# Attention and token-mixing MLP in one kernel: zeroing by DMA and q, k order at the head; DMA latencies in the scheduler's model and matmul order at the tail

## The chip, the cores and the metric

One core of a Trainium2 chip. The metric is device time in microseconds (us), median of several executions. Beside it stands the *span* of the profiler's record, from the first to the last instruction, about 1.8 to 2.2 us shorter. Engines: PE is TensorE, ACT ScalarE, DVE VectorE, POOL GpSimd, SP the queue that issues nearly all DMAs.

## The reference, cut to what matters

```python
xn = layernorm(x)                                  # x: (1, 2048, 512), bf16
qkv = xn @ wqkv                                    # 32 heads of 16
p = softmax(q @ k^T / 4); o = p @ v; A = o @ wo
u = gelu(einsum("bsd,sf->bdf", layernorm(xn), w1) + b1)   # mixes tokens, F = 1376
B = transpose(einsum("bdf,fs->bds", u, w2) + b2)
return x + A + B
```

The scores make 32 heads x 2048 x 2048 exponentials, worked off as 1024 tiles of 128 x 1024.

## The kernel before

The kernel has its own scheduler. It runs through a model of the engines with a cost for every instruction, and from it decides which engine takes which tile and in what order each engine's instructions stand. The order is then fixed; on the chip semaphores alone decide when things start. A tile's exponential is either one ACT instruction, or on DVE an integer approximation of four terms (one from PSUM, three shifts on DVE or POOL). PE sums `P @ V` with the "PV matmuls": a tile from ACT is one group of four 32-column matmuls, a tile from DVE four groups. "PE's backlog" below is what PE still has to do once the last scores are made.

There are 32 blocks of 32 tiles. After each block DVE copies its sums out; DMAs regroup them and the denominators, DVE takes reciprocals, two more DMA steps spread them, and DVE multiplies. Block 31 at the end takes a short way with 32 x 32 transposes.

The head, cut:

```python
sc.add("dve", lambda e: e.memset(v17_main[:, :, 16:17], 1.0), ...)
sc.add("dve", lambda e: e.memset(wo_t[:], 0.0), ..., cost=(0.92, 0.97))
...
for t in range(NPRE):                 # NPRE = 4 tiles of x
    transpose_pe(t, TB[t]); warm_up(N_MID[t], 5)
for t in range(NPRE):
    transpose_copy(t, TB[t], "dve" if t == 2 else "act")
ln_stats(NPRE)
for t in range(NPRE):
    qt0_tile_pe(t)
    if t == 0: kt_tile_pe(0, t, PV_BANK); kt_tile_evac(0, t, PV_BANK, "dve")
    if t == 1: qt0_evac(0, "dve")
for t in range(1, NPRE): kt_tile_pe(0, t, PV_BANK)
qt0_evac(1, "act")
```

DMA in the model, and the tail, cut:

```python
DMA_I, DMA_L, DMA_SLACK = 0.65, 3.0, 0.8        # issue, latency, slack before a use
...
for sti in range(4): heads_of(2, sti)           # pair 14's output matmuls
warm_up(6, ...)
for half in range(2):
    for sti in (half, half + 2):                # block 31's, needs oL of this half
        for a in range(2): matmul(bank(tbk[sti]), lhsT=oL[...], rhs=wo_t[...])
    for sti in (half, half + 2): heads_of(3, sti)     # block 30's
for sti in (0, 2, 1, 3): # DVE (sti 3: ACT) evacuates, DMA out
```

The softmax here doesn't subtract the row's maximum and nothing guards it: scores larger than these inputs give would overflow.

Of the kernel before, what the change touches and what calls it, by code (L numbers as in the profile page):

```python
# [49 lines left out]
N_MID = (1, 1, 1, 2)  # L50
# [4 lines left out]
PER_LIST = 16  # L55
LN2_AT = 12
PIECE_MIN = 6
PIECE_OPEN = 1
HOLD_MAX = 2.0
PE_LAT = 0.40  # L60
# [7 lines left out]
DMA_SLACK = 0.8  # L68
EXT_SLACK = 0.2
# [7 lines left out]
D_BACK = 0.5  # L77
D_STEAL = 0.3
D_LATE = 0.5
P_KEEP = 4  # L80
DEAD_SLACK = 0.1
PAIR_WAIT = 0.0
# [8 lines left out]
LATE_BY = 0  # L91
# [3 lines left out]
FIN_END = 985  # L95
FIN_STEP = 18
# [26 lines left out]
class Sched:  # L123
    ENGS = ("pe", "act", "dve", "pool", "sp")

    def __init__(self, nc, es):
        self.nc = nc
        self.es = es
        self.streams = {e: [] for e in self.ENGS}
        self.order = []  # L130
        self.last_writer = {}
        self.readers = {}
        self.dma_ops = []
        self.free = {e: 0.0 for e in self.ENGS}
        self.busy = {e: 0.0 for e in self.ENGS}
        self.pe_mode = None
        self.pe_end = 0.0
        self.pe_tiles = {}
        self.phase = 0
        self.pieces = {}  # L140
        self.pe_log = []
        self.port_iv = {"dve": [], "pool": []}
        self.port_op = None

# [38 lines left out]
    def _time(self, op, cost, ready, port):  # L183
# [3 lines left out]
        if op.is_dma:  # L187
            op.t0 = max(self.free[eng], ready)
            self.free[eng] = op.t0 + cost[0]
            op.t1 = op.t0 + cost[1]  # L190
# [148 lines left out]
def bass_parallel_sum__softmax_full_mha__mixer_token_mlp__prompt_kernel(  # L339
# [18 lines left out]
    with ExitStack() as es:  # L358
# [70 lines left out]
        def dma(q, dst, src, reads, writes, name="", noncontig=False, out_dma=False):  # L429
            if noncontig:  # L430
                def fn(eng, dst=dst, src=src):
                    with nc.allow_non_contiguous_dma(reason="tiny strided vector load"):
                        return eng.dma_start(dst, src)
            else:
                def fn(eng, dst=dst, src=src):
                    return eng.dma_start(dst, src)  # L436
            return sc.add(q, fn, reads=reads, writes=writes, name=name, dma=True, out_dma=out_dma)
# [13 lines left out]
        sc.add("dve", lambda e: e.memset(wo_t[:], 0.0), writes=[("wo_t", z) for z in range(4)], cost=(0.92, 0.97))  # L451
# [98 lines left out]
        def ln_norm(t):  # L550
            sc.add("dve", lambda e: e.tensor_scalar(xn_sb[:, t, :], x_sb[:, t, :], mv[:, t, 0:1], mv[:, t, 2:3],
                                                    ALU.subtract, ALU.mult),
                   reads=[("x", t), ("mv", t)], writes=[("xn", t)], cost=(0.3, 0.39))
# [114 lines left out]
        for t in range(NPRE):  # L668
            transpose_pe(t, TB[t])
            warm_up(N_MID[t], 5)  # L670
        for t in range(NPRE):
            transpose_copy(t, TB[t], "dve" if t == 2 else "act")
        ln_stats(NPRE)
        for t in range(NPRE):
            qt0_tile_pe(t)
            if t == 0:
                kt_tile_pe(0, t, PV_BANK)
                kt_tile_evac(0, t, PV_BANK, "dve")
            if t == 1:
                qt0_evac(0, "dve")  # L680
        for t in range(1, NPRE):
            kt_tile_pe(0, t, PV_BANK)
        qt0_evac(1, "act")
# [6 lines left out]
        ln_norm(NPRE)  # L690

        def block0_work(period):
            if period == 0:
                for t in range(NPRE):
                    vt_tile_pe(t, 0, 5, t)
                vt_evac(list(range(NPRE)), 0, 5, "dve")
# [19 lines left out]
            if ok(period + 5):  # L716
                ln_stats(period + 5)
            if ok(period + 4) and period:
                ln_norm(period + 4)
# [303 lines left out]
        def task_epilogue(b):  # L1023
            p, e_ = divmod(b, 2)
            qb, T = PAIRS[p]
            eb, tb_ = b % 2, p % 2
            yield "gate", lambda: b < 2 or b - 2 in ot_free
            yield "pvev", [dict(eng="dve", fn=lambda e: e.tensor_copy(OT32[:, eb, :], bank(PV_BANK)),  # L1028
                                reads=[("bank", PV_BANK)], writes=[("OT32", eb)])]
            for c in range(4):  # L1030
                yield "sp", [dict(dst=dcomp[32 * c:32 * c + 32, eb, :],
                                  src=OT32[32 * c + 16:32 * c + 17, eb, :].rearrange("o (c x) -> o c x", x=16),
                                  reads=[("OT32", eb)], writes=[("dcomp", eb, c)], name="den_in")]
# [3 lines left out]
            else:  # L1037
                yield from task_o_in(b)
            yield "dve", [dict(eng="dve", fn=lambda e: e.reciprocal(rcomp[:, eb, :], dcomp[:, eb, :]),
                               reads=[("dcomp", eb, r) for r in range(4)], writes=[("rcomp", eb)], cost=(0.2, 0.25))]  # L1040
            yield "sp", [dict(dst=rden_d[eb].rearrange("(p x) -> p x", x=16), src=rcomp[:, eb, :],
                              reads=[("rcomp", eb)], writes=[("rden_d", eb)], name="den_mid")]
            for r in range(4):
# [5 lines left out]
                                  reads=[("rden_d", eb)], writes=[("denb", tb_, e_, r)], name="den_out")]  # L1049
# [9 lines left out]
            for h in range(2):  # L1059
# [5 lines left out]
                    writes=oT_keys(qb, T) + [("oTh", h)], port=True, cost=(0.33, 0.41))]  # L1065
# [33 lines left out]
        def tail():  # L1099
# [6 lines left out]
            def heads_of(Tm, sti):  # L1106
                sc.add("pe", lambda e: e.matmul(
                    bank(tbk[sti]), lhsT=oT(qb)[:, Tm, 128 * sti:128 * (sti + 1)], rhs=wo_c[:, Tm, :],
                    start=Tm == 2 and sti < 3, stop=Tm == 3),
# [3 lines left out]
            warm_up(6, 2 * slots[1] + 1, wo_c[:, 0, :], wk)  # L1113
            for half in range(2):
                for sti in (half, half + 2):
                    h = sti // 2
                    for a in range(2):
                        sc.add("pe", lambda e, sti=sti, h=h, a=a, half=half: e.matmul(
                            bank(tbk[sti]), lhsT=oL[:, 256 * a + 128 * half:256 * a + 128 * half + 128],
                            rhs=wo_t[:, 2 * h + a, :], start=False, stop=False),  # L1120
                            reads=[("oTl", half)] + [("wo_t", c) for c in range(4)], writes=[("bank", tbk[sti])])
                for sti in (half, half + 2):
                    heads_of(3, sti)
# [145 lines left out]
        def est(specs, slack=0.0):  # L1269
            s0 = specs[0]  # L1270
            r = 0.0
            for s_ in specs:
                r = max(r, sc.ready(s_["eng"], s_["reads"], s_["writes"], slack=slack, dma_slack=DMA_SLACK))
# [28 lines left out]
        def pieces():  # L1302
# [12 lines left out]
            for tries in range(2):  # L1315
# [21 lines left out]
                if len(g["steps"]) >= PIECE_MIN and len(g["open"]) < PIECE_OPEN and g["steps"][-1][1]:  # L1337
# [27 lines left out]
        while True:  # L1365
            cands = []
# [77 lines left out]
            if cur_ext and cur_ext["cur"] and cur_ext["cur"][0] == "hold" and (next_n >= NN or not score_has(next_n)):  # L1444
# [77 lines left out]
            elif kind == "dma":  # L1522
                w = what["cur"][1][0]
                dma("sp", w["dst"], w["src"], w["reads"], w["writes"], w["name"], out_dma=w.get("out_dma", False))
# [133 lines left out]
```

## Time and profile before

| | before |
|---|---|
| device time, median of 3 | 691.98 us (691.9 to 692.06) |
| span of the profile | 690.4 us (its execution took 692.2) |
| ACT: first exponential starts, last one ends | 12.52, 681.87 |
| exponential tiles on ACT, on DVE | 715, 309 |
| final transpose of block 31 starts on DVE | 682.28 |

Read these as four stretches that add up to the span: the head to the first exponential (12.52), ACT's exponentials (669.35, with the GELU between them), from the last one's end to the final transpose (0.41), and the rest (8.12). ACT is nearly gapless in the second; so a stretch gets shorter only if ACT has less to do, or if what is serial at the ends gets shorter.

### The profile page before, as it was taken

The page shows a single profiled execution, that of the slowest core. Times are in us where ns is not written, and L with a number is a line of the kernel's source. Part 1 is how long each engine was busy: PE and PEld are TensorE (multiplying, and loading weights), DVE is VectorE, ACT ScalarE, POOL GpSimd, SP SyncE. Part 2 cuts the span into 40 slices and gives each one's busy share as a digit, 9 for nine tenths or more (in the row PEclk, how much of TensorE's full clock was granted, in tenths as well). Part 3 has the DMA queues.
Part 4 walks back from the last instruction along what each step waited for, and adds up shares of the span by engine and source line. Part 5 has one row for each costly group of instructions (what it writes and reads, how often), then busy time and mean ns, then how long its engine had stood idle before and what let it go on. Part 6 is the DMA issues. An engine that isn't in the chain of part 4 may idle for free.

```text
span 690.4 us, 29398 instructions
## 1 busy us (share of the span) xinstructions
PE 674.3 (98%) x12934; PEld 309.7 (45%) x12934; DVE 618.7 (90%) x895; ACT 672.3 (97%) x734; POOL 401.7 (58%) x690
## 2 busy tenths in 40 slices
PE   7999999999999999999999999999999999999998
PEld 4534544435444454444444444444444444444444
DVE  7989899998889989889999989898998988888987
ACT  5999999999999999999999999999999999999995
POOL 4536557563455756656666576665665665654643
PEclk9999999999999999999999999999999999999999
DMA  7402001221002200022220212222221222313201
GB/s 214 101 5 54 21 18 21 50 45 29 19 18 50 48 20 19 23 52 49 49 42 20 58 29 55 53 55 55 49 49 34 58 53 57 70 28 87 47 22 48
DMA packets 85728, 32.32 MB, mean 47 GB/s; under 512 B 67424, under 2 KB 85600, under 8 KB 85600
## 3 DMA queue, kind: packets, MB, share of 16 engines
q1 hardware_dynamic: 85168, 30.05, 19.1%
q8 instruction: 101, 1.65, 1.1%
q10 hardware_dynamic: 432, 0.39, 0.2%
q14 instruction: 27, 0.22, 0.1%
HBM read 21.76 MB, written 2.35 MB: 35 GB/s over the span
## 4 chain that ended last, share of the span: by engine, by line
PE 78%; ACT 13%; DVE 5%; issue 1%; POOL 1%; SPq 0%; DMA 0%; DVEq 0%
PE ps L811 32%; PE ps L744 28%; PE ps L842 14%; ACT pT L768 10%; ACT x_sb L768 2%; PE ps L896 1%; DVE pT L779 1%; DVE OT L1028 1%; ACT gT_sb L953 1%; DVE hx L567 1%; DVE oT L1061 0%; SPq L436 0%; DMA denb<-rden_scratch 0%; POOL mv L563 0%; PE ps L648 0%
## 5 line engine op out<-in xcount | busy, mean ns | idle before, releaser
L768 ACT ACTIVATE pT<-ps 128x1024 bf16<-128x1024 f32 x535 | 521.1, 1126 | 2.7 <-PE ps L744 2.1
L779 DVE TENSOR_SCALAR pT<-ps 128x1024 int16<-128x1024 f32 x222 | 271.2, 1222 | 28.0 <-PE ps L744 21.2
L744 PE MATMUL ps<-QT,KT 32*128 32x512 bf16 x2048 | 283.1, 384 | 6.0 <-ACT pT L768 3.0
L785 POOL INT64_ADD pT<-pT x319 | 193.0, 613 | 117.1 <-DVE pT L788 77.5
L811 PE MATMUL ps<-pT,V 128*32 128x256 bf16 x4728 | 249.4, 276 | 3.5 <-DVE OT L1028 3.1
L768 ACT ACTIVATE x_sb<-ps 128x1024 bf16<-128x1024 f32 x180 | 194.0, 1130 | 0.6 <-PE ps L744 0.5
L744 PEld LDWEIGHTS ps<-QT,KT 32*128 32x128 bf16 x2048 | 78.2, 91 | 183.7 <-ACT pT L768 69.8
L811 PEld LDWEIGHTS ps<-pT,V 128*32 128x32 bf16 x4728 | 110.3, 96 | 87.3 <-issue 68.8
L785 POOL INT64_ADD x_sb<-pT x142 | 86.6, 613 | 70.0 <-DVE pT L788 32.2
L811 PE MATMUL ps<-x_sb,V 128*32 128x256 bf16 x1840 | 116.4, 275 | 0.7 <-DVE OT L1028 0.4
L779 DVE TENSOR_SCALAR x_sb<-ps 128x1024 int16<-128x1024 f32 x87 | 106.3, 1221 | 8.8 <-PE ps L744 6.7
L785 POOL INT64_ADD pT<-x_sb x115 | 70.1, 618 | 45.7 <-DVE pT L788 27.9
L788 DVE TENSOR_SCALAR pT<-pT 128x1024 int16<-128x1024 int16 x148 | 62.9, 427 | 4.3
L811 PE MATMUL ps<-pT,VM 128*32 128x256 bf16 x888 | 61.6, 274 | 0.0
L842 PE MATMUL ps<-gT_sb,wblk 128*32 128x512 bf16 (+1 forms) x704 | 61.2, 383 | 0.0
L811 PEld LDWEIGHTS ps<-x_sb,V 128*32 128x32 bf16 x1840 | 46.4, 96 | 29.4 <-issue 23.4
L842 PE MATMUL ps<-hx,wblk 128*32 128x512 bf16 x598 | 52.2, 383 | 0.0
L785 POOL INT64_ADD x_sb<-x_sb x55 | 33.4, 612 | 21.7 <-DVE pT L788 11.9
L850 PE MATMUL ps<-hx,wblk 32*128 32x512 bf16 (+1 forms) x92 | 35.6, 387 | 0.0
L788 DVE TENSOR_SCALAR pT<-x_sb 128x1024 int16<-128x1024 int16 x65 | 27.3, 427 | 1.8
L811 PEld LDWEIGHTS ps<-pT,VM 128*32 128x32 bf16 x888 | 23.4, 96 | 9.5 <-issue 8.2
L788 DVE TENSOR_SCALAR x_sb<-pT 128x1024 int16<-128x1024 int16 x57 | 23.9, 420 | 1.5
(111 smaller groups left out, 449.1 us busy)
## 6 DMA issues: line engine op xcount, KB each, us to landing
wblk<-in_B_w_dram SPq DMA_DIRECT2D x10, 512.0 KB, 4.5
wblk<-in_B_w_dram SPq DMA_DIRECT2D x16, 320.0 KB, 3.5
oC<-OT SPq DMA_DIRECT2D x248, 16.0 KB, 1.8
denb<-rden_scratch SPq DMA_DIRECT2D x124, 32.0 KB, 2.3
xr<-in_A_x_dram SPq DMA_DIRECT2D x16, 128.0 KB, 3.5
dcomp<-OT SPq DMA_DIRECT2D x124, 2.0 KB, 1.7
QT<-Qall SPq DMA_DIRECT2D x120, 16.0 KB, 1.8
out_dram<-osb SPq DMA_DIRECT2D x14, 128.0 KB, 2.0
```

Of the source, the lines that this page charges most:

```text
L567: return [dict(eng="dve", fn=lambda e: e.tensor_scalar(xn_sb[:, t, :], xn_sb[:, t, :], mv[:, t, 3:4], None, ALU.mult), reads=[("xn", t), ( ...
L744: specs.append(dict(eng="pe", fn=lambda e, r=r, bk=bk: e.matmul(bank(bk), lhsT=KT[32 * r:32 * r + 32, T, 128 * kt:128 * (kt + 1)], rhs=QT[ ...
L768: return [dict(eng="act", fn=lambda e: e.activation(buf(pbuf[n]), ps[:, s_ * 1024:(s_ + 1) * 1024], ACTF.Exp, scale=LN2_128), reads=[("ban ...
L779: return dict(eng="dve", fn=lambda e: e.tensor_scalar(buf_i(w), ps[:, s_ * 1024:(s_ + 1) * 1024], IBIAS, 0.0, ALU.add, ALU.max), reads=[(" ...
L785: return dict(eng=eng, fn=lambda e: e.int64_add(buf_i(o).bitcast(I64), buf_i(w).bitcast(I64), SHIFTS[k] * 0x0001000100010001), reads=[("pT ...
L788: return dict(eng=eng, fn=lambda e: e.tensor_scalar(buf_i(o), buf_i(w), float(SHIFTS[k]), 1.0, ALU.add, ALU.mult), reads=[("pT", w)], writ ...
L811: specs.append(dict(eng="pe", fn=lambda e, c=c, h=h, i=i, off=off: e.matmul(bank(PV_BANK)[32 * c:32 * c + 32, 256 * par:256 * par + 256], ...
L842: specs.append(dict(eng="pe", fn=lambda e, c=c, w=w: e.matmul(bank(EX_BANK)[32 * c:32 * c + w, :], lhsT=lhs_of(32 * c, 32 * c + w), rhs=rh ...
L850: return [dict(eng="pe", fn=lambda e: e.matmul(bank(EX_BANK)[0:dst_rows, :], lhsT=lhs_of(0, dst_rows)[rs], rhs=rhs[rs], start=begin, stop= ...
L896: return [dict(eng="pe", fn=lambda e, ct=ct, c=c: e.matmul(bank(EX_BANK)[32 * c:32 * c + 32, 128 * i:128 * (i + 1)], lhsT=xnT[:, ct, 128 * ...
L953: yield "act", [dict(eng="act", fn=lambda e, ap=ap: e.activation(ap, ap, ACTF.Gelu_apprx_tanh), reads=[("gT", f) for f in fts], writes=[(" ...
L1028: yield "pvev", [dict(eng="dve", fn=lambda e: e.tensor_copy(OT32[:, eb, :], bank(PV_BANK)), reads=[("bank", PV_BANK)], writes=[("OT32", eb)])]
```

## The change

Intent: take the zeroing of `wo_t` off DVE at the start, let q and k of the first tile run ahead of later transposes, tell the scheduler more truthful DMA latencies, and at the end give block 30's chain short latencies and keep row pieces (matmuls cut in four by rows, slipped in among the scores) away from the last scores.

```diff
-N_MID = (1, 1, 1, 2)
+N_MID = (1, 0, 0, 1)
+PIECE_STOP = 4
+DMA_SLACK_RCP = 1.5
+DMA_SLACK_OT = 2.5
+DMA_BIG = 5.2
+DMA_Q = 2.4
-            op.t1 = op.t0 + cost[1]
+            op.t1 = op.t0 + max(cost[1], DMA_BIG - (op.t0 - self.big))   # self.big: last w1 or w2 load
-        sc.add("dve", lambda e: e.memset(wo_t[:], 0.0), ...)
+        def zero_wo_t():            # in period 4 of block 0, from a zeroed part of QT
+            dma("sp", wo_t[:], QT[:, 3:4, :].to_broadcast([128, 4, 512]), ...)
@@ head: copy right after each transpose; tile 0's q and k after transpose 1
+            if t == 1: qt0_tile_pe(0); kt_tile_pe(0, 0, PV_BANK)
+        for t in range(1, NPRE - 1): qt0_tile_pe(t)
+        qt0_tile_pe(NPRE - 1)
+        kt_tile_evac(0, 0, PV_BANK, "dve"); qt0_evac(0, "act"); qt0_evac(1, "act")
@@ epilogue of a block
+            quick = b == NBLK - 2;  dc = (DMA_I, DMA_Q) if quick else None    # cost of its DMAs
+            dma_slack=0.0 if quick else DMA_SLACK if b >= NBLK - 4 else DMA_SLACK_RCP (or _OT)
@@ pieces: only while next_n < NN - PIECE_STOP
@@ tail
             warm_up(6, ...)
+            for sti in range(4): heads_of(3, sti)
             for half in range(2): ... # block 31's eight matmuls, with no heads_of(3) between
```

(Cut: ten sets of scheduling rules, all chosen as set 0, which has the old constants; a rule that lets other PE work go before held pieces; names and unused switches.)

More of the change, by code (lines that the diff above doesn't have):

```diff
@@ L55 @@
 PER_LIST = 16
+SEG = 8
+RULES = (
+    (0.5, 0.5, 0.3, 0.0, 6, 0),
+    (0.3, 0.5, 0.3, 0.0, 6, 0),
+    (0.8, 0.5, 0.3, 0.0, 4, 0),
+    (0.5, 0.8, 0.3, 0.0, 6, 0),
+    (0.5, 0.5, 0.45, 0.15, 6, 0),
+    (0.5, 0.5, 0.15, 0.0, 4, 0),
+    (0.5, 0.35, 0.3, 0.3, 4, 0),
+    (0.8, 0.8, 0.3, 0.0, 99, 0),
+    (0.5, 0.5, 0.3, 0.0, 4, 6),
+    (0.5, 0.8, 0.45, 0.1, 4, -6),
+)
+RULE_OF = "00000000000000000000000000000000000000000000000000000000000000000000000000000000000000000000000000000000000000000000000000000000"
 LN2_AT = 12
-PIECE_MIN = 6
 PIECE_OPEN = 1
 HOLD_MAX = 2.0
+ZERO_AT = 4
+POOL_NORM = ()
+STATS_LEAD = 0
+N_LAST = 0
+Q0_ENG = "act"
 PE_LAT = 0.40
@@ L76 @@
 D_FLY = 3
-D_BACK = 0.5
-D_STEAL = 0.3
-D_LATE = 0.5
 P_KEEP = 4
 DEAD_SLACK = 0.1
-PAIR_WAIT = 0.0
 PORT_SLACK = 0.5
@@ L90 @@
 HARD_HOLD = 10
-LATE_BY = 0
 EX_FROM = 34
@@ L143, in __init__ @@
         self.port_op = None
+        self.big = -9.0
     def _deps(self, eng, reads, writes, dma):
@@ L189, in _time @@
             self.free[eng] = op.t0 + cost[0]
-            op.t1 = op.t0 + cost[1]
+            op.t1 = op.t0 + max(cost[1], DMA_BIG - (op.t0 - self.big))
+            if op.name in ("ld_w1", "ld_w2a"):
+                self.big = op.t0
         elif eng == "pe":
@@ L427, in bass_parallel_sum__softmax_full_mha__mixer_token_mlp__prompt_kernel, with dma @@
         H_KEYS = [("xn", t) for t in range(NT)]
-        def dma(q, dst, src, reads, writes, name="", noncontig=False, out_dma=False):
+        def dma(q, dst, src, reads, writes, name="", noncontig=False, out_dma=False, cost=None):
             if noncontig:
@@ L436, in fn @@
                     return eng.dma_start(dst, src)
-            return sc.add(q, fn, reads=reads, writes=writes, name=name, dma=True, out_dma=out_dma)
+            return sc.add(q, fn, reads=reads, writes=writes, name=name, dma=True, out_dma=out_dma, cost=cost)
         sc.add("pool", lambda e: e.memset(ident[:], 0.0), writes=[("ident",)], cost=(0.25, 0.3))
@@ L450, in bass_parallel_sum__softmax_full_mha__mixer_token_mlp__prompt_kernel @@
         sc.add("dve", lambda e: e.memset(v17_main[:, :, 16:17], 1.0), writes=[("Vone",)], cost=(0.5, 0.55))
-        sc.add("dve", lambda e: e.memset(wo_t[:], 0.0), writes=[("wo_t", z) for z in range(4)], cost=(0.92, 0.97))
         sc.add("pool", lambda e: e.memset(qmask[:, 0:1], 0.0), writes=[("qmask",)], cost=(0.1, 0.2))
@@ L550, in ln_norm @@
         def ln_norm(t):
-            sc.add("dve", lambda e: e.tensor_scalar(xn_sb[:, t, :], x_sb[:, t, :], mv[:, t, 0:1], mv[:, t, 2:3],
+            pool = t in POOL_NORM
+            sc.add("pool" if pool else "dve", lambda e: e.tensor_scalar(xn_sb[:, t, :], x_sb[:, t, :], mv[:, t, 0:1], mv[:, t, 2:3],
                                                     ALU.subtract, ALU.mult),
-                   reads=[("x", t), ("mv", t)], writes=[("xn", t)], cost=(0.3, 0.39))
+                   reads=[("x", t), ("mv", t)], writes=[("xn", t)], cost=(2.09, 2.2) if pool else (0.3, 0.39), port=pool)
         def ln2_stats():
@@ L669, in bass_parallel_sum__softmax_full_mha__mixer_token_mlp__prompt_kernel @@
             transpose_pe(t, TB[t])
+            transpose_copy(t, TB[t], "dve" if t == 2 else "act")
             warm_up(N_MID[t], 5)
-        for t in range(NPRE):
-            transpose_copy(t, TB[t], "dve" if t == 2 else "act")
-        ln_stats(NPRE)
-        for t in range(NPRE):
-            qt0_tile_pe(t)
-            if t == 0:
-                kt_tile_pe(0, t, PV_BANK)
-                kt_tile_evac(0, t, PV_BANK, "dve")
-            if t == 1:
-                qt0_evac(0, "dve")
+            if t == 1:
+                qt0_tile_pe(0)
+                kt_tile_pe(0, 0, PV_BANK)
+        for t in range(1, NPRE - 1):
+            qt0_tile_pe(t)
+        warm_up(N_LAST, 5)
+        qt0_tile_pe(NPRE - 1)
+        kt_tile_evac(0, 0, PV_BANK, "dve")
+        qt0_evac(0, Q0_ENG)
+        qt0_evac(1, "act")
+        ln_stats(NPRE)
         for t in range(1, NPRE):
             kt_tile_pe(0, t, PV_BANK)
-        qt0_evac(1, "act")
         evac("dve", KT[:, 0, 128:512], bank(PV_BANK)[:, 128:512], reads=[("bank", PV_BANK)],
@@ L690, in bass_parallel_sum__softmax_full_mha__mixer_token_mlp__prompt_kernel @@
         ln_norm(NPRE)
+        for t in range(NPRE + 1, NPRE + 1 + STATS_LEAD):
+            ln_stats(t)
+        def zero_wo_t():
+            dma("sp", wo_t[:], QT[:, 3:4, :].to_broadcast([128, 4, 512]),
+                reads=[("QT", 3, r) for r in range(4)], writes=[("wo_t", z) for z in range(4)], name="zero")
         def block0_work(period):
+            if period == ZERO_AT:
+                zero_wo_t()
             if period == 0:
@@ L715, in block0_work @@
                 vt_tile_pe(period + 2, 0, 5, period % 2)
-            if ok(period + 5):
-                ln_stats(period + 5)
-            if ok(period + 4) and period:
+            if ok(period + 5 + STATS_LEAD):
+                ln_stats(period + 5 + STATS_LEAD)
+            if ok(period + 5) and period + 5 in POOL_NORM:
+                ln_norm(period + 5)
+            if ok(period + 4) and period and period + 4 not in POOL_NORM:
                 ln_norm(period + 4)
@@ L1026, in task_epilogue @@
             eb, tb_ = b % 2, p % 2
+            quick = b == NBLK - 2
+            dc = (DMA_I, DMA_Q) if quick else None
             yield "gate", lambda: b < 2 or b - 2 in ot_free
@@ L1032, in task_epilogue @@
                                   src=OT32[32 * c + 16:32 * c + 17, eb, :].rearrange("o (c x) -> o c x", x=16),
-                                  reads=[("OT32", eb)], writes=[("dcomp", eb, c)], name="den_in")]
+                                  reads=[("OT32", eb)], writes=[("dcomp", eb, c)], name="den_in", cost=dc)]
             g_in = dict(gen=task_o_in(b), cur=None)
@@ L1039, in task_epilogue @@
             yield "dve", [dict(eng="dve", fn=lambda e: e.reciprocal(rcomp[:, eb, :], dcomp[:, eb, :]),
-                               reads=[("dcomp", eb, r) for r in range(4)], writes=[("rcomp", eb)], cost=(0.2, 0.25))]
+                               reads=[("dcomp", eb, r) for r in range(4)], writes=[("rcomp", eb)], cost=(0.2, 0.25), dma_slack=0.0 if quick else DMA_SLACK if b >= NBLK - 4 else DMA_SLACK_RCP)]
             yield "sp", [dict(dst=rden_d[eb].rearrange("(p x) -> p x", x=16), src=rcomp[:, eb, :],
-                              reads=[("rcomp", eb)], writes=[("rden_d", eb)], name="den_mid")]
+                              reads=[("rcomp", eb)], writes=[("rden_d", eb)], name="den_mid", cost=dc)]
             for r in range(4):
@@ L1048, in task_epilogue @@
                                   src=src.to_broadcast([16, 2, 256]),
-                                  reads=[("rden_d", eb)], writes=[("denb", tb_, e_, r)], name="den_out")]
+                                  reads=[("rden_d", eb)], writes=[("denb", tb_, e_, r)], name="den_out", cost=dc)]
             half = b == NBLK - 2
@@ L1064, in task_epilogue @@
                           [("denb", tb_, x, r) for x in es_ for r in range(4)],
-                    writes=oT_keys(qb, T) + [("oTh", h)], port=True, cost=(0.33, 0.41))]
+                    writes=oT_keys(qb, T) + [("oTh", h)], port=True, cost=(0.33, 0.41),
+                                   dma_slack=0.0 if quick else DMA_SLACK if b >= NBLK - 4 else DMA_SLACK_OT)]
             yield "call", lambda: oT_done.add((qb, T))
@@ L1108, in heads_of @@
                     bank(tbk[sti]), lhsT=oT(qb)[:, Tm, 128 * sti:128 * (sti + 1)], rhs=wo_c[:, Tm, :],
-                    start=Tm == 2 and sti < 3, stop=Tm == 3),
+                    start=Tm == 2 and sti < 3, stop=False),
                     reads=[("oTc", qb, 2) if Tm == 2 else ("oTh", sti // 2)] + wk, writes=[("bank", tbk[sti])])
@@ L1113, in tail @@
             warm_up(6, 2 * slots[1] + 1, wo_c[:, 0, :], wk)
+            for sti in range(4):
+                heads_of(3, sti)
             for half in range(2):
@@ L1119, in tail @@
                             bank(tbk[sti]), lhsT=oL[:, 256 * a + 128 * half:256 * a + 128 * half + 128],
-                            rhs=wo_t[:, 2 * h + a, :], start=False, stop=False),
+                            rhs=wo_t[:, 2 * h + a, :], start=False, stop=a == 1),
                             reads=[("oTl", half)] + [("wo_t", c) for c in range(4)], writes=[("bank", tbk[sti])])
-                for sti in (half, half + 2):
-                    heads_of(3, sti)
             for sti in (0, 2, 1, 3):
@@ L1272, in est @@
             for s_ in specs:
-                r = max(r, sc.ready(s_["eng"], s_["reads"], s_["writes"], slack=slack, dma_slack=DMA_SLACK))
+                r = max(r, sc.ready(s_["eng"], s_["reads"], s_["writes"], slack=slack, dma_slack=s_.get("dma_slack", DMA_SLACK)))
             t = max(sc.free[s0["eng"]], r)
@@ L1336, in pieces @@
                         break
-                if len(g["steps"]) >= PIECE_MIN and len(g["open"]) < PIECE_OPEN and g["steps"][-1][1]:
+                if len(g["steps"]) >= piece_min and len(g["open"]) < PIECE_OPEN and g["steps"][-1][1] and next_n < NN - PIECE_STOP:
                     g["open"].append((g["steps"].pop(-1)[1], {0, 1, 2, 3}))
@@ L1365, in bass_parallel_sum__softmax_full_mha__mixer_token_mlp__prompt_kernel @@
         while True:
+            D_LATE, D_BACK, D_STEAL, PAIR_WAIT, piece_min, LATE_BY = RULES[int(RULE_OF[min(next_n, NN - 1) // SEG])]
             cands = []
@@ L1443, in bass_parallel_sum__softmax_full_mha__mixer_token_mlp__prompt_kernel @@
                 jobs.append((max(t_c, est(cur_ext["cur"][1], EXT_SLACK)), 1 if late > -LATE_BY else 3, "ext", cur_ext, 0.214))
-            if cur_ext and cur_ext["cur"] and cur_ext["cur"][0] == "hold" and (next_n >= NN or not score_has(next_n)):
+            held = cur_ext and cur_ext["cur"] and cur_ext["cur"][0] == "hold" and (next_n >= NN or not score_has(next_n))
+            if held and jobs and min(j[0] for j in jobs) < max(max(sc.piece_ready(r) for o in cur_ext["open"] for r in o[1]), t_pe) + 0.2:
+                held = False
+            if held:
                 for o in cur_ext["open"]:
@@ L1523, in bass_parallel_sum__softmax_full_mha__mixer_token_mlp__prompt_kernel @@
                 w = what["cur"][1][0]
-                dma("sp", w["dst"], w["src"], w["reads"], w["writes"], w["name"], out_dma=w.get("out_dma", False))
+                dma("sp", w["dst"], w["src"], w["reads"], w["writes"], w["name"], out_dma=w.get("out_dma", False), cost=w.get("cost"))
                 step_gen(what)
```

## The prediction

> **What bounds the kernel now.** I first read busy time by engine, then who waits for whom on ScalarE, then the timelines of the head and the tail.
>
> ```profile
> PE 674.3 (98%) x12934; PEld 309.7 (45%) x12934; DVE 618.7 (90%) x895; ACT 672.3 (97%) x734; POOL 401.7 (58%) x690
> ...
> L768 ACT ACTIVATE pT<-ps 128x1024 bf16<-128x1024 f32 x535 | 521.1, 1126 | 2.7 <-PE ps L744 2.1
> L779 DVE TENSOR_SCALAR pT<-ps 128x1024 int16<-128x1024 f32 x222 | 271.2, 1222 | 28.0 <-PE ps L744 21.2
> ...
> L768 ACT ACTIVATE x_sb<-ps 128x1024 bf16<-128x1024 f32 x180 | 194.0, 1130 | 0.6 <-PE ps L744 0.5
> ```
>
> There are 1024 score tiles. ScalarE takes 535 + 180 = 715 with a true exponential, VectorE 222 + 87 = 309 with the integer trick. PE's 98% is pipelined time and proves little. ScalarE's row is decisive: its 715 exponentials sat idle 2.7 + 0.6 = 3.3 us in total, so from the first to the last of them ScalarE is the bound. VectorE is idle some 70 us, 28.0 + 8.8 of it waiting for scores. ScalarE's own timeline has its other idle time, at both ends:
>
> ```profile
> 7.18 0.60 ACT L573 ACTIVATE xnT<-ps 128x512 bf16<-128x512 bf16 x1 [2.27 <-PE ps L579]
> ...
> 9.88 0.60 ACT L573 ACTIVATE xnT<-ps 128x512 bf16<-128x512 bf16 x1 [0.77 <-PE ps L579]
> 11.56 0.47 ACT L640 ACTIVATE QT<-ps,qmask 128x256 bf16<-128x256 f32 x1 [1.09 <-DVE QT L643]
> 12.52 3.77 ACT L768 ACTIVATE pT<-ps 128x1024 bf16<-128x1024 f32 x4 [0.48 <-PE ps L744]
> ```
>
> ```profile
> 674.28 7.59 ACT L768 ACTIVATE pT<-ps 128x1024 bf16<-128x1024 f32 x8
> ```
>
> (Columns: start, duration, engine and line, and in brackets the idle time before and its releaser.) The first exponential starts at 12.52; the last ends at 674.28 + 7.59 = 681.87. So 690.4 = 12.5 head + 669.4 of exponentials (with the GELU between) + 8.5 tail. In runs of eight, their pitch is (7.59 - 1.13) / 7 = 0.92 us.
>
> What delays the first exponential, on VectorE:
>
> ```profile
> 2.84 0.48 DVE L450 MEMSET V<- 128x512 bf16 x1 [1.70 <-issue]
> ...
> 3.47 0.91 DVE L451 MEMSET wo_t<- 128x1024 uint32 x1
> ...
> 4.30 0.63 DVE L521 BATCH_NORM_STATS2 stats<-x_sb 128x6 f32<-128x512 bf16 x1
> ...
> 8.52 0.87 DVE L551 TENSOR_SCALAR hx<-x_sb,mv 128x512 bf16<-128x512 bf16 x1 [0.17 <-POOL mv L531]
> ...
> 10.98 0.48 DVE L643 TENSOR_SCALAR QT<-ps,qmask 128x256 bf16<-128x256 f32 x1
> ```
>
> The statistics of the first x tile wait behind the zeroing of wo_t although x is there: ScalarE reads its tile at 3.43 after a 0.27 us DMA wait, and x DMAs land 2.6 us after issue at 0.7. Then all goes serially to the normalization of tile 3, its transpose and copy, q and k, the evacuation of q's first half on VectorE (10.98) and of the second on ScalarE (11.56, waiting for the first), scores, 12.52.
>
> The tail, VectorE again:
>
> ```profile
> 682.28 0.72 DVE L1086 STREAM_TRANSPOSE denb<-ps 128x512 f32<-128x512 f32 x1 [0.86 <-PE ps L811]
> ...
> 684.49 0.38 DVE L1061 TENSOR_TENSOR wkv_raw<-oC,denb 64x256 bf16<-64x256 f32 x1
> 684.80 0.41 DVE L1095 TENSOR_TENSOR oT<-ps,oC 128x256 bf16<-128x256 f32 x1
> 685.13 0.41 DVE L1061 TENSOR_TENSOR wkv_raw<-oC,denb 64x256 bf16<-64x256 f32 x1
> ...
> 687.10 0.69 DVE L1130 SCALAR_TENSOR_TENSOR osb<-ps,hx 128x512 bf16<-128x512 f32 x1 [0.21 <-PE ps L1107]
> ```
>
> The two multiplies of block 30 (L1061) sit inside block 31's final chain, after VectorE had idled 0.86 us ahead of it.
>
> **What the Trainium skill says.** "VectorE: DVE Perf Modes", section "Zero memsets can be issued as uint32 (trn2)": a memset takes one cycle per element whatever the type. The trace agrees that elements count: 1024 take 0.91 us, 256 take 0.27. At the page's 0.96 GHz 1024 would be 1.07 us; the trace's 0.91 stands.
> "SBUF — State Buffer", "SBUF: two separate sides": VectorE and GpSimd share a port pair under an exclusive lock. The trace shows tile 3's normalization at 0.87 us instead of 0.41 while GpSimd's VM memsets run (8.43 to 9.24). In the new order both move together, so this loss should stay.
> "DMA: Bandwidth & Descriptors", "Anatomy of one DMA": a fixed cost of about 2.0 us. The trace has 1.7 to 2.3 us medians for block 30's kinds of transfer; the scheduler had assumed 3.0 us plus 0.8 slack, so the diff's 2.4 us for this block is realistic.
>
> **The change part by part.**
> (1) Zeroing wo_t: minus 0.91 us on VectorE, ahead of everything in the head. The new DMA reads zeros from QT slot 3. It is queued ahead of the wo loads, and these behind the small b1 load that holds the queue till 16.7; the zeros are written by GpSimd at about 17 to 18 us. It delays those loads by perhaps 2 us; the w1 loads end up about 2 us later, still far from first use after 45 us. Hidden.
> (2) q and k of tile 0 ahead of the transposes 2 and 3, both q evacuations on ScalarE, three warm-up matmuls fewer. Timeline, worked by hand with the durations above: statistics of tile 0 at 3.45 (not 4.30); normalization 0 ends 5.84; the 13 untouched warm-ups still end near 5.9, so transpose 0 is at about 5.95; normalization 3 ends 8.55; transpose 3, then q of tiles 1 and 2; ScalarE copies tile 3 at 9.0 to 9.6, evacuates q's first half to 10.1 and, q of tile 3 being ready at about 10.05, the second to 10.55. Scores at 10.6, first exponential at 11.05 instead of 12.52: **minus 1.45 us**, of which about 0.85 is the memset and 0.6 the reordering. VectorE's program up to v's evacuation gets 0.91 + 0.48 = 1.39 us shorter, so it keeps up through block 0.
> (3) The middle. The ten "rules" are all rule 0, equal to the old constants, so that machinery is inert. New DMA slacks let the reciprocal and the oT multiplies come later in VectorE's order, as the old ones idled 3.8 + 1.0 us there. The order of instructions after the change holds 712 exponentials on ScalarE (was 715) and 312 on VectorE (was 309). Three exponentials at 0.92 us: **minus 2.75 us** of ScalarE. VectorE pays 3 x 1.22 and saves 3 shifts of 0.43 (GpSimd does 12 more at 0.61, being 58% busy): plus 2.4 us, out of 70 idle.
> (4) The tail. Both L1061 multiplies now precede the final transpose, where VectorE had 0.86 us idle. The second L1095 moves from 684.80 to about 684.5, and the eight wo_t matmuls run without waiting for L1061. The half-1 results are then complete near 686.2 instead of 686.9 to 687.3; the three VectorE evacuations start at 685.3, 685.9 and 686.55 instead of 687.10: **minus 0.55 us** counted from the last PV matmul.
> (5) No row pieces at the end: the last feed-forward tile is finished in whole steps. By the order, 84 PV matmuls and 24 others (was 56 and none) follow the last score. In groups of four at 0.11 and 0.22 us this is 21 x 0.11 + 6 x 0.22 = 3.6 us against 14 x 0.11 = 1.5 us. Before, the last score (680.05) was 2.2 us ahead of the final transpose; now it will be nearly 4. Part is backlog which an earlier last score allows; I charge **plus 1.2 us**, a choice between 0 and 1.8.
> Sum: -1.45 - 2.75 - 0.55 + 1.2 = -3.55 us.
>
> **The rivals.** (A) PE takes over as the bound in the last 5 us: the full 1.8 us of (5) or more is lost, and of the three saved exponentials little arrives. For it: the counts of (5), and PE gaps of only 0.1 to 0.2 us. Against: ScalarE waited 3.3 us in the whole middle. Result about 690.
> (B) Block 30's denominators arrive late. With the multiplies ahead of the final transpose, a late DMA now holds the whole tail. In the new queue order reciprocals go out after three oC transfers, not five; with issues of about 0.6 us, about 12 us pass from the OT copy to landing, and VectorE has about 13 us of work between. Tight: up to 1 us lost, result 689 to 689.5.
> (C) The changed order makes new waits in the middle: VectorE or PE slip and ScalarE idles more than 3.3 us. Every microsecond is lost directly; 1 to 2 us are possible, and could as well be won.
> (D) The head gain is hidden: x tiles or weights land too late. Against: by the median landing times the first-slice q weights are in by 5.7 and x tiles 0 to 3 by 4 us, all before use.
>
> **Range and chances.** 692.0 - 3.55 = 688.45; I say 688.4. All gains intact and no PE backlog gives 687.2, less with luck in the middle: low end 686.3. Rivals A and B together with a little of C give 690.7. Two per cent is 13.8 us; nothing here is near it in either direction. Runs before agree within 0.2 us, so the sign should be clear.
>
> **What would show it.** First exponential at 10.9 to 11.3, VectorE's first statistics at about 3.45. Exponential rows of 712 and 312, idle before ScalarE's still about 3 us; more means C. Last exponential ending at about 677.5 to 678; the final transpose 2 us (A) or less than 0.5 us after it. L1086's counterpart released by PE is mine, L1061's counterpart released by a DMA is B. From the final transpose to the end 7.5 instead of 8.1 us. The prediction is wrong if ScalarE gains more than 4 us of idle time in the middle, or if the head stays at 12 us.

## The result, and the profile after

The changed kernel took **689.72 us** (median of 4 runs, 689.6 to 689.8) against 691.96: ratio 0.9967, 95% interval 0.995 to 0.9985. Ratios here are the mean time of one kernel's runs over that of the other's of the same rounds, so not quite the ratio of the medians. It is a real gain of 2.2 us, inside the predicted range (686.3 to 690.7), and 1.3 us short of the predicted 688.4.

The page of the kernel after, busy time and the exponentials' groups (the last number ahead of the releaser is idle time before them):

```profile
PE 674.2 (98%) x12966; PEld 310.9 (45%) x12966; DVE 620.9 (90%) x893; ACT 669.4 (97%) x732; POOL 407.9 (59%) x702
...
L800 ACT ACTIVATE pT<-ps 128x1024 bf16<-128x1024 f32 x513 | 502.6, 1122 | 2.8 <-PE ps L776 2.1
L811 DVE TENSOR_SCALAR pT<-ps 128x1024 int16<-128x1024 f32 x229 | 279.6, 1221 | 22.7 <-PE ps L776 16.2
...
L800 ACT ACTIVATE x_sb<-ps 128x1024 bf16<-128x1024 f32 x199 | 213.9, 1130 | 0.3 <-PE ps L776 0.2
```

513 + 199 = 712 on ACT, idle 3.1 us: ACT is still the bound of the middle. DVE's idle time before its own is 22.7 + 9.2 us, from 28.0 + 8.8.

The head on ACT, then on DVE, after:

```profile
9.34 0.60 ACT L594 ACTIVATE xnT<-ps 128x512 bf16<-128x512 bf16 x1 [0.82 <-PE ps L600]
9.84 1.07 ACT L661 ACTIVATE QT<-ps,qmask 128x256 bf16<-128x256 f32 x2
11.43 3.77 ACT L800 ACTIVATE pT<-ps 128x1024 bf16<-128x1024 f32 x4 [0.52 <-PE ps L776]
```

```profile
3.53 0.69 DVE L541 BATCH_NORM_STATS2 stats<-x_sb 128x6 f32<-128x512 bf16 x1 [0.21 <-DMA x_sb<-in_A_x_dram]
...
7.93 0.92 DVE L572 TENSOR_SCALAR hx<-x_sb,mv 128x512 bf16<-128x512 bf16 x1 [0.17 <-POOL mv L551]
```

The first exponential starts at 11.43, not 12.52. The statistics now wait for the DMA of x, not for a memset.

The tail on DVE after:

```profile
677.42 0.86 DVE L1095 TENSOR_TENSOR wkv_raw<-oC,denb 64x256 bf16<-64x256 f32 x2
679.91 0.72 DVE L1121 STREAM_TRANSPOSE denb<-ps 128x512 f32<-128x512 f32 x1 [1.64 <-PE ps L843]
...
683.46 0.69 DVE L1165 SCALAR_TENSOR_TENSOR osb<-ps,hx 128x512 bf16<-128x512 f32 x1 [0.79 <-PE ps L1155]
```

Block 30's products are now ahead of the transpose, as intended, and no DMA holds them. But DVE then idles 1.64 us for PE, and later 0.79 us, again for PE. The chain that ended last shows PE from the last score on (start, duration, what); first before, then after:

```profile
680.13 0.32 PE ps L744 x2
680.45 1.78 PE ps L811 x56
682.22 0.97 PE ps L1107 x4
```

```profile
675.84 0.32 PE ps L776 x2
676.15 0.22 PE ps L843 x4
676.38 0.22 PE ps L874 x4
676.60 0.11 PE ps L843 x4
676.70 1.08 PE ps L874 x20
677.78 2.08 PE ps L843 x76
679.86 0.97 PE ps L1142 x4
680.83 1.29 PE ps L669 x6
682.12 0.86 PE ps L1142 x4
682.99 1.74 PE ps L1155 x8
```

ACT's last exponential ended at 676.20 + 1.15 = 677.35 (before: 681.87). The four stretches, in us:

| stretch | before | after | change | predicted |
|---|---|---|---|---|
| to the first exponential | 12.52 | 11.43 | -1.09 | -1.45 |
| first to last exponential | 669.35 | 665.92 | -3.43 | -2.75 |
| last exponential to final transpose | 0.41 | 2.56 | +2.15 | +1.2 |
| final transpose to end | 8.12 | 8.09 | -0.03 | -0.55 |
| sum = span | 690.4 | 688.0 | -2.40 | -3.55 |

ACT finished 4.5 us earlier; 2.2 of them were given back to PE's backlog.

### The profile page after: what moved, and what is told of

Read it like the earlier page. It is cut to its first block, busy times and chain, and to the rows that moved or that the text cites. A ratio compares the mean times of both kernels' runs of the same rounds, so it can differ in the third digit from the quotient of the medians.

```text
span 688.0 us, 29503 instructions
## 1 busy us (share of the span) xinstructions
PE 674.2 (98%) x12966; PEld 310.9 (45%) x12966; DVE 620.9 (90%) x893; ACT 669.4 (97%) x732; POOL 407.9 (59%) x702
## 4 chain that ended last, share of the span: by engine, by line
PE 60%; ACT 34%; DVE 3%; issue 1%; POOL 1%; DMA 0%; DVEq 0%
PE ps L843 25%; ACT pT L800 23%; PE ps L776 22%; PE ps L874 11%; ACT x_sb L800 10%; PE ps L928 1%; ACT gT_sb L985 1%; DVE pT L811 1%; DVE hx L588 1%; POOL mv L584 0%; DVE OT L1062 0%; DMA x_sb<-in_A_x_dram 0%; PE ps L669 0%; DVE x_sb L811 0%; PE ps L600 0%
## 5 line engine op out<-in xcount | busy, mean ns | idle before, releaser
L800 ACT ACTIVATE pT<-ps 128x1024 bf16<-128x1024 f32 x513 | 502.6, 1122 | 2.8 <-PE ps L776 2.1
L811 DVE TENSOR_SCALAR pT<-ps 128x1024 int16<-128x1024 f32 x229 | 279.6, 1221 | 22.7 <-PE ps L776 16.2
L817 POOL INT64_ADD pT<-pT x339 | 205.0, 613 | 115.9 <-DVE pT L820 68.3
L843 PE MATMUL ps<-pT,V 128*32 128x256 bf16 x4732 | 245.4, 275 | 1.8 <-DVE OT L1062 1.3
L800 ACT ACTIVATE x_sb<-ps 128x1024 bf16<-128x1024 f32 x199 | 213.9, 1130 | 0.3 <-PE ps L776 0.2
L817 POOL INT64_ADD x_sb<-pT x135 | 82.2, 612 | 68.0 <-DVE pT L820 32.0
L811 DVE TENSOR_SCALAR x_sb<-ps 128x1024 int16<-128x1024 f32 x83 | 101.4, 1221 | 9.2 <-PE ps L776 6.6
L817 POOL INT64_ADD x_sb<-x_sb x51 | 31.1, 614 | 18.0 <-DVE pT L820 10.7
L820 DVE TENSOR_SCALAR x_sb<-pT 128x1024 int16<-128x1024 int16 x64 | 27.3, 428 | 2.0
L820 DVE TENSOR_SCALAR pT<-x_sb 128x1024 int16<-128x1024 int16 x59 | 25.2, 429 | 1.5
```

The source lines that it names most:

```text
L800: return [dict(eng="act", fn=lambda e: e.activation(buf(pbuf[n]), ps[:, s_ * 1024:(s_ + 1) * 1024], ACTF.Exp, scale=LN2_128), reads=[("ban ...
L811: return dict(eng="dve", fn=lambda e: e.tensor_scalar(buf_i(w), ps[:, s_ * 1024:(s_ + 1) * 1024], IBIAS, 0.0, ALU.add, ALU.max), reads=[(" ...
L817: return dict(eng=eng, fn=lambda e: e.int64_add(buf_i(o).bitcast(I64), buf_i(w).bitcast(I64), SHIFTS[k] * 0x0001000100010001), reads=[("pT ...
L820: return dict(eng=eng, fn=lambda e: e.tensor_scalar(buf_i(o), buf_i(w), float(SHIFTS[k]), 1.0, ALU.add, ALU.mult), reads=[("pT", w)], writ ...
L843: specs.append(dict(eng="pe", fn=lambda e, c=c, h=h, i=i, off=off: e.matmul(bank(PV_BANK)[32 * c:32 * c + 32, 256 * par:256 * par + 256], ...
```

## The experiments

Twelve runs, each timed in five rounds. Runs 1 to 4, 5 to 8 and 9 to 12 each shared a chip and nine runs of the kernel before, with medians of 691.96, 692.19 and 692.11 us. Stretches are from each run's profile:

| run | time | ratio to before | first exp. | middle | gap to transpose | rest |
|---|---|---|---|---|---|---|
| 1 old head | 691.61 | 0.9994 | 12.51 | 666.29 | 2.57 | 8.03 |
| 2 memset back | 690.65 | 0.9981 | 12.01 | 665.91 | 2.56 | 8.02 |
| 3 old DMA latencies | 691.26 | 0.9990 | 11.26 | 669.28 | 0.39 | 8.87 |
| 4 tail, fewer warm-ups | 688.89 | 0.9955 | 11.17 | 665.91 | 2.56 | 7.16 |
| 5 changed kernel again | 689.75 | 0.9964 | 11.39 | 665.92 | 2.57 | 8.02 |
| 6 VM zeroed later | 689.21 | 0.9957 | 10.80 | 665.92 | 2.57 | 8.01 |
| 7 runs 4 and 6 together | 688.29 | 0.9944 | 10.77 | 665.92 | 2.56 | 7.25 |
| 8 run 7, MLP due earlier | **687.66** | **0.9934** | 11.08 | 665.86 | 1.62 | 7.14 |
| 9 old slacks only | 693.46 | 1.0020 | 11.47 | 669.39 | 2.86 | 8.08 |
| 10 no short latencies | 690.16 | 0.9972 | 11.27 | 666.59 | 2.06 | 8.08 |
| 11 old tail order | 689.61 | 0.9964 | 11.46 | 665.94 | 2.57 | 7.93 |
| 12 row pieces to the end | 690.82 | 0.9982 | 11.31 | 665.93 | 2.14 | 9.62 |

The middle repeats to about 0.02 us where the order of instructions is the same (2, 4, 5, 6, 7, 12). The first exponential does not, since the arrival of x varies: ACT read its first x tile between 3.37 us (run 6) and 3.81 us (run 11). In runs 4 and 8 the chain into the first exponential does not go back to x at all but to the warm-up matmuls at PE's start: the last of the thirteen ended at 6.91 us (run 7: 6.08).

**Run 1: the old head on the changed kernel.**

```diff
-N_MID = (1, 0, 0, 1)
+N_MID = (1, 1, 1, 2)
+        sc.add("dve", lambda e: e.memset(wo_t[:], 0.0), ...)
# transposes, q, k and their evacuations in the order of the kernel before; no zeroing DMA
```

> The changed kernel with the old head (wo_t zeroed on VectorE, old order of q and k, old warm-ups); the order of the middle and of the tail is unchanged, 712 exponentials on ScalarE and 312 on VectorE. Theory (the head's gain passes one to one into the end): first exponential back at 12.5 us instead of 11.4, time 1.1 us above the changed kernel, 690.8. Rival (the head's gain is taken back later, because PE's backlog sets the end): under 0.4 us, 690.1 or less.

The first exponential went to 12.51, and the gap to the transpose stayed at 2.57 us: the head's gain passes whole into the end, and the rival falls. The time rose by more than the head's 1.1 us. The middle was 0.37 us longer with the same order of instructions. The traces place this in one spot: the 90th exponential (96.96 us) starts 0.37 us late, as its scores waited for DVE, and DVE had stood idle 0.50 us ahead of a multiply (93.70 us). The kernel before has the same stall (0.49 us, at 93.69); in every run with the new head it is 0.13 us. So the new head is worth this 0.37 us as well; what DVE stood for, the profile does not show. The time also exceeded the span by 2.16 us (run 5: 1.85), for which I have no cause.

**Run 2: only the memset back.**

```diff
+        sc.add("dve", lambda e: e.memset(wo_t[:], 0.0), ...)
-            if period == ZERO_AT:
-                zero_wo_t()
```

> The changed kernel with only the memset of wo_t put back on VectorE and the zeroing DMA taken out; new head order kept. If the memset alone delays the statistics, first exponential at 11.43 + (4.30 - 3.53) = 12.2 us and time 0.75 us above the changed kernel, 690.5; if the x transfer now bounds the head, the memset should cost less than its 0.91 us, as 0.2 to 0.3 us of it hide behind the wait for x. Rival: the reordering is the whole gain, then under 0.3 us.

Statistics at 4.29, first exponential at 12.01: 0.6 us of the head is the memset and, from 12.01 to run 1's 12.51, 0.5 us the new order. The 0.91 us instruction yields only 0.6 because x arrives too late to use the rest, as the 0.21 us wait for the DMA above shows. This share moves with x: in runs 3 and 10, whose x was read as early as here (3.56 and 3.57 us; changed kernel 3.73), the first exponential is at 11.26 and 11.27, so that the memset costs 0.74 us. The time, 690.65, is 0.9 above the changed kernel's, but the span only 0.6 (688.5 against 687.9 in run 5); as in run 1, time exceeds span by 0.3 us more than usual.

**Run 3: the old DMA latencies.**

```diff
-DMA_SLACK_RCP = 1.5
-DMA_SLACK_OT = 2.5
-DMA_BIG = 5.2
+DMA_SLACK_RCP = 0.8
+DMA_SLACK_OT = 0.8
+DMA_BIG = 0.0
-            quick = b == NBLK - 2
+            quick = False
```

> The changed kernel with the old DMA latencies in the scheduler's model (flat 3.0 us and 0.8 slack, no short latencies for block 30); head, piece rule and tail order stay new. Its order has 715 exponentials on ScalarE and 309 on VectorE, and 56 PV matmuls with no other work after the last score, as the kernel before. Theory: the latencies alone make the middle's gain and the backlog: from first to last exponential about 669.3 us (changed: 665.9), last exponential to final transpose 0.4 us (changed: 2.6), so the net is only 1.2 us: 690.9. Rival (the middle's gain is from less waiting, not from the three exponentials): span of the exponentials stays near 666.5.

As the theory had it: 715 exponentials, a middle of 669.28, a gap of 0.39 us. So the latencies in the model make both the middle's gain and the backlog behind it. One thing was not expected: the rest grew to 8.87 us, because block 30's products fell back into the final chain while the new matmul order has PE wait for them ahead of block 31's matmuls.

**Run 4: block 30's output matmuls ahead of the warm-ups, one warm-up instead of six.**

```diff
-            warm_up(6, 2 * slots[1] + 1, wo_c[:, 0, :], wk)
             for sti in range(4):
                 heads_of(3, sti)
+            warm_up(1, 2 * slots[1] + 1, wo_c[:, 0, :], wk)
```

> The changed kernel with block 30's four output matmuls ahead of the warm-up ones at the end, and one warm-up matmul instead of six. Theory (in the changed kernel PE reaches the wo_t matmuls 0.7 us after their input is ready, because the warm-ups hold it till 681.75 and the four matmuls follow): first wo_t matmul right after the first product, the last output 0.7 us earlier, 689.0. Rival (VectorE's three evacuations or the output transfers set the end): no more than 0.1 us.

688.89; from the transpose to the end 7.16 instead of 8.09 us. On PE, from the final transpose (679.64) on:

```profile
679.75 1.67 PE ps L1142 x7
681.42 0.22 PE ps L669
...
681.64 0.62 PE ps L1155 x2
```

Block 31's first matmul runs 2.0 us after the transpose starts. In the changed kernel it ran 2.9 us after it (682.82 on the timeline, against 679.91), held by 1.29 us of warm-ups and then by the four matmuls. This wait on PE ate the predicted gain of the tail. The run changes the order and the number of the warm-ups at once; which of the two gives how much is not shown.

**Run 5: the changed kernel again.** No edit.

> The changed kernel once more, as a control for the runs of the first set, whose times were 0.2 to 0.5 us higher than their profiles' spans let one expect. If chips or sets differ by that much: 689.9 to 690.1. If not: 689.7. Its profile also tells whether the late x tile of the first profile (read by ScalarE at 3.73 us, in the other runs 3.48 to 3.63) was chance: then the first exponential is near 11.2 instead of 11.43.

689.75, the same as the first time: sets and chips agree within about 0.1 us. ACT read x at 3.70 again and the first exponential was at 11.39. So the late x was no single accident, and the control refutes my guess of 11.2.

**Run 6: GpSimd zeroes VM later.**

```diff
-        zero_memsets("VM", VM, vm_kh)
         ...
         ln_stats(NPRE)
+        zero_memsets("VM", VM, vm_kh)
```

> The changed kernel with GpSimd's zeroing of VM moved behind the statistics of tile 4, so that it no longer runs while VectorE normalizes tile 3. Theory (tile 3's normalization takes 0.92 us instead of 0.41 because GpSimd's memsets hold the shared port, and lies on the head's chain): its duration 0.41, first exponential 0.5 us earlier (10.7 to 10.9), time 0.5 us below the changed kernel. Rival (the duration has another cause, or the head has a second chain just behind): under 0.15 us.

```profile
7.77 0.41 DVE L572 TENSOR_SCALAR hx<-x_sb,mv 128x512 bf16<-128x512 bf16 x1 [0.18 <-POOL mv L551]
```

0.41 instead of 0.92 us, first exponential at 10.80: the memsets had stretched the normalization, and it lies on the chain. About 0.14 of the 0.6 us is an x that came earlier in this run: the first normalization ended at 5.93 instead of 6.07 (run 5). The time fell by 0.54 us against run 5.

**Run 7: both mends.** The edits of runs 4 and 6.

> Both mends together: output matmuls of block 30 ahead with one warm-up matmul, and the late zeroing of VM. They lie at the two ends, so they should add: 0.8 + 0.5 = 1.3 us below the changed kernel, 688.4. If the head's gain is swallowed by PE's backlog at the end, only 0.8.

688.29, 1.46 us below run 5 on the same chip: head and tail gains add, and nothing is swallowed.

**Run 8: run 7 with the MLP's last tiles due earlier.**

```diff
-FIN_END = 985
+FIN_END = 950
```

> The kernel of e7 with the feed-forward tiles due earlier (the last one by score 950 instead of 985): the same 712 and 312 exponentials and the same total of matmuls, but after the last score 84 PV matmuls and 4 others instead of 84 and 24. Theory (PE has become a second bound: work taken from behind the last score only pushes the scores back): last exponential 0.5 to 1 us later, gap to the final transpose 1 us shorter, time within 0.4 us of e7. Rival (the backlog is bad placement alone): last exponential as in e7, time 1.1 us less (5 groups of four at 0.22).

```profile
675.56 0.32 PE ps L776 x2
675.88 0.22 PE ps L843 x4
676.11 0.22 PE ps L874 x4
676.32 2.18 PE ps L843 x80
678.51 1.83 PE ps L1142 x8
```

My theory fell. The gap shrank by 0.94 us, while the middle stayed at 665.86: PE had room for those 20 matmuls among the scores. Part of the backlog was placement alone. The time fell by 0.63 us; 0.3 us of the gain was lost in the head, to warm-up matmuls that ended at 6.91 instead of 6.08 us and held the transposes. This is the fastest version, 687.66 us, 4.5 below the kernel before and correct.

**Run 9: only the two new slacks back at 0.8.**

```diff
-DMA_SLACK_RCP = 1.5
-DMA_SLACK_OT = 2.5
+DMA_SLACK_RCP = 0.8
+DMA_SLACK_OT = 0.8
```

> The changed kernel with only the two new slacks (reciprocal 1.5, products 2.5) back at 0.8. Its order has 717 exponentials on ScalarE and 307 on VectorE, 80 PV matmuls and 32 others after the last score. Theory (the length of the middle is the number of ScalarE's exponentials): from first to last exponential 665.9 + 5 x 0.92 = 670.5 us, up to 671.5 if the step from 715 to 712 (3.4 us) is taken as the rate; time 4 us or more above the changed kernel, slower than the kernel before. Rival (the middle is set by waits): within 1.5 us of the changed kernel's 665.9.

Slower than the kernel before, as expected, but the middle is 669.39, not 670.5 or more. It has two exponentials more than run 3 and is only 0.1 us longer; 1.0 us of the difference is that it idles 2.4 us before them instead of 3.4. The count is the main term, not the only one. The run also parts two things: without the new slacks the middle's gain is gone, but the backlog stays (gap 2.86 us), although DVE has fewer tiles than in the kernel before.

**Run 10: no short latencies for block 30.**

```diff
-            quick = b == NBLK - 2
+            quick = False
```

> The changed kernel without the short latencies for block 30 (the general new latencies stay). Its order still has 712 and 312 and still has both of block 30's products ahead of the final transpose; 88 PV matmuls and 12 others follow the last score instead of 84 and 24. Theory (the short latencies matter little, the general ones make the gain): middle 665.9, gap to the transpose 0.3 to 0.5 us shorter, time 689.2 to 689.6. Rival (block 30's chain then comes late): products wait for their transfer, final transpose up to 1 us later, 690.5.

690.16, between the two forecasts. The gap is 0.5 us shorter, the middle 0.67 us longer (idle 3.5). Block 30's products remain ahead of the transpose. The longer middle is two late exponentials near its end (at 671.06 and 672.26, by 0.54 and 0.28 us), whose scores PE made behind 20 feed-forward matmuls. The short latencies are worth some 0.4 us, and not through block 30's chain.

**Run 11: the old order of the last matmuls.** The four `heads_of(3)` go back behind each half of block 31's matmuls.

```diff
-            for sti in range(4):
-                heads_of(3, sti)
+                for sti in (half, half + 2):      # inside the loop over halves
+                    heads_of(3, sti)
```

> The changed kernel with the old order of the last matmuls (block 30's output matmuls after each half of block 31's), all else new. Theory (the new order only moves the wait from VectorE to PE): from the final transpose to the end within 0.15 us of the changed kernel's 8.05, time 689.6 to 689.9. Rival (the new order is worth the 0.5 us that I predicted): 8.5 us and 690.2.

7.93 and 689.61: the new matmul order alone is worth nothing.

**Run 12: row pieces to the last score.**

```diff
-PIECE_STOP = 4
+PIECE_STOP = 0
```

> The changed kernel with row pieces allowed to the last score. 712 and 312 stay; 84 PV matmuls and 20 others follow the last score instead of 84 and 24. Theory (the piece rule is not what makes PE's backlog): gap from the last exponential to the final transpose 0.2 us shorter at most, time within 0.3 us of the changed kernel. Rival (the rule makes the backlog): gap shorter by 1 us or more.

The gap was 0.43 us shorter, twice what I allowed, but the time rose by 1.1 us against run 5, outside both forecasts. The loss is where neither looked, after the transpose (chain of the last PE work; the transpose starts at 679.38):

```profile
677.25 2.08 PE ps L843 x76
679.32 0.33 PE ps L882
...
679.70 0.40 PE ps L882
...
680.15 0.38 PE ps L882
680.53 0.33 PE ps L874 x4
680.86 0.97 PE ps L1142 x4
```

Three pieces were left over when the scores ended. They run one after the other, each waiting for the one before, 0.44 us apart, and with the last whole step they push all of the tail's matmuls back by over 1 us.

## Why the prediction was right or wrong

The range held. That ACT bounds the middle, that the head's gain is passed on, that three exponentials fewer are worth about 3 us and that PE's backlog takes part of it back was named rightly; how the tail would gain and where the backlog comes from was not. Part of the agreement is luck: head, tail and backlog came out 1.8 us worse than predicted together, and the middle 0.7 us better for reasons that the prediction did not have. Rival A came nearest: the whole backlog was charged and the net was 689.7, as it said; but the three saved exponentials did arrive, which it denied. Rival B did not happen: no DMA held the products. Rival C did not: ACT's idle time stayed at 3.1 us.

Taken by its own steps:

1. *Zeroing by DMA is hidden.* Right. It was issued at 17.3 us, after the small b1 load that holds the queue, and landed 3.7 us later. The w1 loads were issued from 24.9 instead of 22.7 us, and the first 80 exponentials start at the same distances from the first one as before, within 0.02 us.
2. *Head, -1.45.* It measured -1.09. The step that failed is "statistics of tile 0 at 3.45" together with "normalization 0 ends 5.84": statistics started at 3.53 and normalization 0 ended at 6.11. DVE's moments waited till 5.24 for ACT's sums of tile 1, which ended at 5.21, as ACT had read the tile only at 3.73. I took one arrival time from one profile for a fixed number; with the memset gone, x's arrival had become the bound. Run 6 shows the same head at 10.80 when x is early and tile 3's normalization is not stretched.
3. *Middle, -2.75.* It measured -3.43. Starts that follow at once are 0.904 us apart in the traces (for instance 103.77 and 104.67 in the changed kernel), so three exponentials are 2.7 us. The other 0.7 us is lateness: what the starts lose beyond this pitch adds up to 22.7 us before and 22.0 after. Of this, 0.37 us is the stall that went with the old head (run 1); the rest I can't place. Recorded idle time fell by only 0.2 us: an exponential lasts 1.13 us and overlaps the next, which can start 0.2 us late without any idle time. Run 9 warns against counting alone (its lateness is 21.0 us, run 3's 22.6).
4. *Tail, -0.55.* It measured -0.03. The step that failed is "the eight wo_t matmuls run without waiting for L1061". They do run without it, but I did not check what stands ahead of them on PE: six warm-ups of 1.29 us and then the four block-30 matmuls. DVE's wait had become PE's. Run 4 moves them and gets the gain, and more (0.9 us).
5. *Backlog, +1.2.* It measured +2.15. My own count, 3.6 us of PE work against 1.5 us, was about right (PE's chain: 0.22 + 0.22 + 0.11 + 1.08 + 2.08 = 3.7 us against 1.78). The step that failed is "Part is backlog which an earlier last score allows": the last score ran 1.5 us ahead of the last exponential's end, no earlier than in the kernel before (1.7 us), so the full difference came. I also gave the wrong reason. The rule on row pieces makes 0.43 us of the gap but saves 1.6 us behind it, 1.1 us in the time (run 12). The backlog comes with the new latencies (run 3). It does not come from the three tiles moved to DVE, although they mean nine more groups of PV matmuls: run 9 has 307 tiles on DVE and 24 PV matmuls fewer than the kernel before, and still 80 PV matmuls and 32 others behind the last score. Which constant puts them there is not shown; `DMA_BIG` is the one that runs 9 and 10 have in common with the changed kernel. Run 8 shows that about 1 us can be hidden by placement.

## What to carry to other kernels

Once a serial wait is taken out, ask what arrives next: here a 0.91 us memset was worth 0.6, because what came behind it then waited for data that landed late. When the engine that bounds a stage finishes earlier, look at what another engine still has to do after the last item: it stands at the end in full, and where it is placed matters as well as how much it is. And for an in-order engine, check the whole queue ahead of an instruction, fillers included, before claiming that it starts when its input is ready.

## What the Trainium skill lacked or had wrong

- "VectorE: DVE Perf Modes", section "Zero memsets can be issued as uint32 (trn2)", gives one cycle per element; at the page's clock of 0.96 GHz that is an estimate of 1.04 ns. The trace's 1024 and 256 elements took 0.912 and 0.272 us: (0.912 - 0.272) / 768 = 0.83 ns per element, faster than the page has it.
- "SBUF — State Buffer", section "SBUF: two separate sides", was confirmed and is worth using: moving GpSimd's memsets of VM cut a normalization from 0.92 to 0.41 us (run 6). It says that the blocked side waits for the other's whole instruction, and not what happens when that side has more of them queued: the delay of 0.51 us is nearer two of the 0.31 us memsets than one.
- "DMA: Bandwidth & Descriptors", section "Anatomy of one DMA — SWDGE (gpsimd) path", fits a DMA's time by size for the path through GpSimd only. The DMAs here are issued by SP and ACT, for which I found no such fit: the zeroing transfer of 512 KB took 3.7 us. Nor is a spread given: the same 128 KB load of x was in use between 3.37 and 3.81 us in these runs, and that moved the first exponential.
- No page gives the cost of leftover pieces that write one bank (it belongs to "TensorEngine Tiling (Array Packing)"): three row-tile matmuls into it, made to wait for each other, ran 0.44 us apart (run 12), against 0.22 us for a group of four column tiles.
